# Chunks of x 64 bytes further apart, for gate and fill, in an attention and MoE kernel

## The chip, the cores and the metric

The kernel runs on one core of one Trainium2 chip. The metric is the device time of one execution in microseconds (us): 1310.79 us before the change, the median of three runs (1310.79 to 1315.36). An execution with the hardware profiler on gives the profile. Its engines are PE (matmul; PEld is its weight load), DVE, ACT, POOL and SP.

## The reference

```
phi(x)  = [exp(p), exp(-p)],  p = x @ w_phi - max|x @ w_phi|
kv      = phi(k)^T v,  z = sum phi(k)              # per batch and head
attn    = phi(q) kv / (phi(q) z + 1e-6)            # 8 x 8 heads, 576 x 64
x       = attn as 4608 tokens x 512                # then the MoE part
xn      = x / rms(x) * rms_g
out     = (silu(xn @ w_gate) * (xn @ w_val)) @ w_out   # 512 -> 1536 -> 512
```

All of it is float32. Every product of two matrices is split into a high and a low part of each factor and made of three products: high x high, high x low, low x high.

## The kernel before, in words

The work has three stages that overlap a little. In *attention* pairs of heads go through `front`, `mid`, `back` and `last`; `last` stores x, transposed, to the DRAM tensor `xs` (512 x 4608). x has 512 rows, so a contraction over them takes four chunks of 128 partitions: NC = 4.

*Fill* uses PE time between and after the attention work. `fill` takes a block of 256 tokens (TF; 18 blocks), splits it into high and low parts in the tile `xo`, and makes the first three of the twelve columns of 128 of gate and of val without the division by rms: six outputs a block, called units. Each is a sum of twelve products of 256 columns (L482): four chunks c, three products each. They go to DRAM by way of the tile `fo`.

*Gate* works on blocks of 512 tokens (T; NB = 9). `prep` makes x / rms * g, and `parts` splits it into the tile `xb`, high and low parts of four chunks. `gv` makes the other nine columns j of gate and of val: for each of two a sum of twelve products of 512 columns (L625). `hidden` applies silu on ACT and the product on DVE, and stores to `hs`.

*The output stage* loads `hs` as `ht` in groups of 256 tokens, forms seven sums and differences of quarter blocks (a11, a12, s1 to s4, a22), splits them, and makes seven products (L805), each a sum over kp = 0 to 5 of three products of 256 columns with the output weights `wh0` to `wh5` and `wl0` to `wl5`. These are split by `split_o` near the end of gate; `wh5` is the last.

In a matmul call the first operand is loaded as weights (stationary) and the second streams through (moving). In fill and gate the moving operand is a chunk of x; in the output stage it is a weight tile, and the stationary one a part of `ht`.

What is behind what: each engine runs its instructions in order. The order is set when the program is built, by the order of the code, by `late()`, which holds instructions back, and by a scheduler that simulates the program. Tiles lie in pools, one behind the other in a partition. When a pool is closed, the next ones take its place, and a new tile waits until the last reader of an old one beneath it is done. The two tiles `xb` lie in the pools `xo0` and `xo1`, and blocks take turns; blocks 0, 2, 4, 6 and 8 use `xo0`.

Addresses, by the built program, in bytes from the start of a partition: `xo` starts at 60192 and 68384, `xb` at 68384 and 101152, all 32 mod 256. A chunk of `xb` is 512 floats or 2048 bytes, one of `xo` 256 floats or 1024 bytes, so all chunks start at 32 mod 256. The weights of fill and gate start at 32 mod 256 too, and so do the stationary operands of the output stage. `wh0` to `wh3` and `wl0` to `wl3` start at 224 mod 256, `wh4`, `wl4`, `wh5` and `wl5` at 32. In attention the moving operands `wh` and `wl` of L319 to L321 start at 96 mod 256, and `qh` and `ql` of L423 at 32 for the first half of the columns and at 160 for the second, each against stationary operands at 32.

Of the kernel before, what the change touches and what calls it, by code (L numbers as in the profile page):

```python
# [9 lines left out]
F32R = mybir.dt.float32r  # L10
# [48 lines left out]
def _split(nc, hi, lo, x, hi_copy=None, lo_eng=None):  # L59
    (hi_copy or nc.scalar.copy)(hi, x)  # L60
    (lo_eng or nc.vector).tensor_tensor(lo, x, hi.bitcast(F32), ALU.subtract)  # L61
# [21 lines left out]
def kernel(ctx: ExitStack, tc: tile.TileContext, q, k, v, w_phi,  # L83
# [5 lines left out]
    NC, NJ = DM // 128, DF // 128  # L89
# [8 lines left out]
    T = 512  # L98
    NB = N // T
    TF = 256  # L100
# [65 lines left out]
        return ri  # L166

    def parts(bk, x, ri):
        xhl = xops[bk % len(xops)].tile([128, 2, NC, T], F32R, name="xb")
        for c in range(0, NC, 2):  # L170
            _split(nc, *(a[:, c:c + 2] for a in (xhl[:, 0], xhl[:, 1], x)), lo_eng=nc.gpsimd)
        return xhl[:, 0], xhl[:, 1], ri
# [7 lines left out]
    @contextmanager  # L180
    def late():

        ins = nc.cur_bb.bb.instructions
        n = len(ins)
        with ExitStack() as es:
            for eng in LATE:
                for i in reversed(ins[-300:]):
                    if i.engine == eng and i.name not in waiting:
                        es.enter_context(tc.issue_after(i))
                        break  # L190
            yield
        waiting.update(i.name for i in nc.cur_bb.bb.instructions[n:])
# [3 lines left out]
    xfp = a_ctx.enter_context(tc.tile_pool(name="a_xf", bufs=2))  # L196
# [269 lines left out]
    blocks = list(range(N // TF))  # L466

    def fill(bk, x):
        xhl = xfp.tile([128, 2, NC, TF], F32R, name="xo")
        xx = dict(h=xhl[:, 0], l=xhl[:, 1])  # L470
        with late():
            for c in range(0, NC, 2):
                _split(nc, *(a[:, c:c + 2] for a in (xx["h"], xx["l"], x)))

        def unit(j, wi):
            js = slice(j * 128, (j + 1) * 128)
            fp = ps_s.tile([128, 512], F32, name="sm") if ended else ps_f.tile([128, T], F32, name="fp")
            i = 0
            for c in range(NC):
                a, al = wf1[wi][0][:, c, js], wf1[wi][1][:, c, js]  # L480
                for w, x in ((a, "h"), (a, "l"), (al, "h")):
                    nc.tensor.matmul(fp[:, 0:TF], w, xx[x][:, c], start=(i == 0), stop=(i == 3 * NC - 1))  # L482
                    i += 1
            o = xfp.tile([128, TF], F32, name="fo", bufs=6)
            nc.scalar.copy(o, fp[:, 0:TF])
            (nc.scalar if tail else nc.sync).dma_start(out=gvv[j][:, wi, bk * TF:(bk + 1) * TF], in_=o)
        return [lambda j=j, wi=wi: unit(j, wi) for j in range(J1) for wi in range(2)]
# [13 lines left out]
    def landed():  # L501
        if here:
            units.extend(fill(*here.pop(0)))
# [63 lines left out]
    def own(name, bufs=1):  # L567
        return g_ctx.enter_context(tc.tile_pool(name=name, bufs=bufs, reuse_waits="tile"))
# [3 lines left out]
    xops = [own("xo0"), xo1]  # L572
# [106 lines left out]
    split_gv(1)  # L679
    raw = raw_load(0, 0)  # L680
    xb = {0: parts(0, x0, ri0)}

    LAST = [*range(JL, JN), 4, 5, *range(4)]
    for bk in range(NB):
        for n, j in enumerate(LAST if bk == NB - 1 else range(JN)):
            gv(bk, j)
            m, k = divmod(n, JN // J1)
            if k == 1:
                with late():
                    gv_raw(bk, m, raw)  # L690
            if k == 2 and (m + 1 < J1 or bk + 1 < NB):
                raw = raw_load(bk, m + 1) if m + 1 < J1 else raw_load(bk + 1, 0)
            if n == 0 and bk + 1 < NB:
                xn = fetch(bk + 1)
            if n == 2 and bk + 1 < NB:
                with late():
                    rin = prep(bk + 1, xn, *((ps_f, "fp") if bk else (ps_g, "gp")))
                xb[bk + 1] = parts(bk + 1, xn, rin)
            if bk and n % 2 == 0 and decs:
                decs.pop(0)()  # L700
            if wot and n % 4 == 0:
                with late():
                    wos_ops.append(split_o(len(wos_ops), rg, wot))
                wot = None
            if not decs and not wot and len(wos_ops) < PRE and n % 4 == 1:
                wot = fetch_o(len(wos_ops))
# [170 lines left out]
```

## Time and profile before

| | |
|---|---|
| median of three runs | 1310.79 us |
| the profiled execution | 1314.92 us, span 1313.0 us |
| mean granted TensorE clock | 0.996 of full speed |
| PE busy | 1277.2 us (97%) |
| DVE, ACT, POOL busy | 840.1 us (64%), 706.1 us (54%), 626.7 us (48%) |
| gate's first and last product (L625) | 499.7 and 1046.3 us |
| fill's first and last product (L482) with val weights | 196.3 and 623.5 us |

The busy time of an engine counts every moment in which at least one of its instructions runs. Products are pipelined: one is still draining while the next streams in, so that the mean duration of one (389 ns with 512 columns) is longer than the time from one start to the next. The chain of waits is followed back from the last instruction, and what it says of a line is time that passed on that line alone. A tile's name stands without its number in these rows: `wh<-wc` may be any of the six.

### The profile page before, as it was taken

Reading aid. Unit: us, or ns where it says so; the run is one execution under the profiler, and the core shown is the slowest. Engines: PE = TensorE matmul, PEld = TensorE weight load, DVE = VectorE, ACT = ScalarE, POOL = GpSimd, SP = SyncE. Lnnn points to the kernel's source line nnn. Section 1 sums busy time; section 2 is a strip of 40 time slices with the busy share of each in tenths; the row PEclk is TensorE's granted clock in tenths of the full one; section 3 lists DMA queues with packets and bytes.
Section 4 is the critical chain, followed back from the end, with each engine's and each line's share of the span. In section 5 each row is a group of like instructions: output and inputs, shape, how many; then the busy total and the mean of one; then the engine's idle time right before and its main releaser. Section 6 shows DMA issues by size and latency. Waiting matters only on the chain.

```text
span 1313.0 us, 24159 instructions
## 1 busy us (share of the span) xinstructions
PE 1277.2 (97%) x8886; PEld 1188.5 (91%) x8886; DVE 840.1 (64%) x1228; ACT 706.1 (54%) x1472; POOL 626.7 (48%) x580
## 2 busy tenths in 40 slices
PE   7989999999999998999999999999999999999998
PEld 7989999999999897999888888888888899999998
DVE  7989888787788962320245645644545786687773
ACT  6978887787778874543243443442332444444442
POOL 4666655565555854200414223223211277776774
PEclk9999999999999999999999999999999999999999
DMA  5545565566656436643446435434425544445541
GB/s 162 132 128 149 163 183 147 149 179 173 179 158 176 126 95 187 201 153 118 147 142 208 147 130 196 150 126 158 144 87 164 182 144 149 143 131 160 159 129 48
DMA packets 198228, 197.12 MB, mean 150 GB/s; under 512 B 69024, under 2 KB 154912, under 8 KB 198112
## 3 DMA queue, kind: packets, MB, share of 16 engines
q1 hardware_dynamic: 169024, 172.26, 43.5%
q10 hardware_dynamic: 29088, 23.34, 5.9%
q8 instruction: 70, 1.15, 0.4%
q14 instruction: 46, 0.38, 0.1%
HBM read 126.04 MB, written 69.50 MB: 149 GB/s over the span
## 4 chain that ended last, share of the span: by engine, by line
PE 80%; DVE 8%; DMA 5%; ACT 3%; issue 2%; SPq 1%; POOL 1%; ACTq 0%; DVEq 0%; POOLq 0%
PE gp L625 18%; PE gq L625 15%; PE gd L805 6%; PE gy L805 6%; PE gz L805 6%; PE sm L482 6%; PE acc L359 4%; PE fp L482 4%; PE sm L423 3%; PE fp L805 3%; PE fp L423 2%; PE pp L321 2%; PE pp L319 2%; DVE mx L323 2%; PE pp L320 1%
## 5 line engine op out<-in xcount | busy, mean ns | idle before, releaser
L388 POOL TENSOR_TENSOR ql<-eq,qh 128x256 fp32r<-128x256 f32 x256 | 218.2, 884 | 54.3 <-issue 31.1
L608 DVE TENSOR_TENSOR h<-sl,gp 128x512 f32<-128x512 f32 x81 | 55.4, 685 | 169.5 <-PE gp L625 159.2
L625 PE MATMUL gp<-xb,wv 128*128 128x512 f32 x648 | 157.8, 389 | 0.0
L625 PEld LDWEIGHTS gp<-xb,wv 128*128 128x128 f32 x648 | 121.1, 188 | 24.7
L625 PE MATMUL gq<-xb,wg 128*128 128x512 f32 x576 | 139.0, 389 | 0.0
L54 POOL TENSOR_TENSOR wa<-raw,wa 128x192 f32<-128x192 f32 (+1 forms) x112 | 67.1, 622 | 137.7 <-DVE wa L52 70.4
L61 POOL TENSOR_TENSOR xb<-x,xb 128x1024 fp32r<-128x1024 f32 x18 | 45.9, 2572 | 180.5 <-ACT xb L60 180.5
L359 PE MATMUL acc<-vm,ek 128*128 128x65 f32 x1024 | 130.3, 269 | 0.0
L625 PEld LDWEIGHTS gq<-xb,wg 128*128 128x128 f32 x576 | 108.1, 188 | 22.5
L359 PEld LDWEIGHTS acc<-vm,ek 128*128 128x128 f32 x1024 | 126.5, 192 | 0.5 <-ACT ek L346 0.4
L323 DVE TENSOR_REDUCE mx<-pp 128x4 f32<-128x512 f32 (+1 forms) x160 | 100.7, 630 | 30.3 <-PE pp L321 29.0
L384 ACT ACTIVATE qh<-sm 128x512 fp32r<-128x512 f32 (+1 forms) x192 | 97.0, 505 | 0.0
L319 PE MATMUL pp<-wh,th 128*128 128x256 f32 x288 | 88.9, 310 | 4.8 <-ACT th L60 1.5
L606 ACT ACTIVATE sl<-gq 128x512 f32<-128x512 f32 x72 | 42.7, 593 | 84.3 <-PE gq L625 80.3
L383 ACT ACTIVATE eq<-sm 128x512 f32<-128x512 f32 x128 | 78.3, 612 | 14.8 <-PE sm L372 11.6
L321 PE MATMUL pp<-wh,tl 128*128 128x256 f32 x288 | 84.5, 300 | 0.1
L320 PE MATMUL pp<-wl,th 128*128 128x256 f32 x288 | 81.5, 284 | 0.0
L625 PE MATMUL gp<-xb,fv 128*128 128x512 f32 x324 | 77.8, 389 | 0.0
L346 ACT ACTIVATE ek<-yk 128x512 f32<-128x512 f32 x128 | 75.1, 647 | 1.1 <-DVE yk L326 1.1
L154 POOL TENSOR_TENSOR ss<-ss,sq 128x512 f32<-128x512 f32 x27 | 34.8, 1289 | 79.7 <-ACT sq L153 79.7
L625 PEld LDWEIGHTS gp<-xb,fv 128*128 128x128 f32 x324 | 60.8, 188 | 12.6
L625 PE MATMUL gq<-xb,fg 128*128 128x512 f32 x288 | 69.2, 389 | 0.0
(210 smaller groups left out, 3802.9 us busy)
## 6 DMA issues: line engine op xcount, KB each, us to landing
hs<-h SPq DMA_DIRECT2D x108, 256.0 KB
ht<-hs SPq DMA_DIRECT2D x18, 1536.0 KB
gvr<-gvs SPq DMA_DIRECT2D x27, 512.0 KB
rc<-di SPq DMA_DIRECT2D x32, 288.0 KB
x<-xs ACTq DMA_DIRECT2D x18, 512.0 KB
x<-xs SPq DMA_DIRECT2D x9, 1024.0 KB
gvs<-fo ACTq DMA_DIRECT2D x70, 128.0 KB
kt<-in_k_dram SPq DMA_DIRECT2D x32, 256.0 KB
```

The costliest lines, as they stand in the source:

```text
L319: nc.tensor.matmul(o, th[:, cs], wh, start=True, stop=False)
L320: nc.tensor.matmul(o, th[:, cs], wl, start=False, stop=False)
L321: nc.tensor.matmul(o, tl[:, cs], wh, start=False, stop=True)
L323: nc.vector.tensor_reduce(mx[:, 0:2 * m], pp[:, 0:2 * m], axis=AX.X, op=ALU.max, apply_absolute_value=True)
L346: nc.scalar.activation(e[h][:, sg], y["k", h], AF.Exp, scale=1.0 - 2.0 * sg)
L359: nc.tensor.matmul(acc[:, sg, h], e[h][:, sg, j], vm[:, h, j], start=False, stop=(h == 1 and j == T0 - 1))
L383: nc.scalar.activation(ei[:, sg], yi, AF.Exp, scale=1.0 - 2.0 * sg)
L384: nc.scalar.activation(hi[:, sg], yi, AF.Exp, scale=1.0 - 2.0 * sg)
L388: nc.gpsimd.tensor_tensor(lo[:, sg, cs], ei[:, sg, cs], hi[:, sg, cs].bitcast(F32), ALU.subtract)
L482: nc.tensor.matmul(fp[:, 0:TF], w, xx[x][:, c], start=(i == 0), stop=(i == 3 * NC - 1))
L625: nc.tensor.matmul(gp[:, 0:T], w, e[:, c], start=(i == 0), stop=(i == 3 * NC - 1))
L805: nc.tensor.matmul(place[n], a[:, kp], w[:, o], start=(first and kp == 0 and i == 0), stop=(kp == KP - 1 and i == 2), skip_group_check=True)
```

## The change

Both tiles of x's parts get rows that are 16 floats longer, and only the first T or TF columns of a row are used.

```
     def parts(bk, x, ri):
-        xhl = xops[bk % len(xops)].tile([128, 2, NC, T], F32R, name="xb")
+        xhl = xops[bk % len(xops)].tile([128, 2, NC, T + 16], F32R, name="xb")[:, :, :, 0:T]
...
     def fill(bk, x):
-        xhl = xfp.tile([128, 2, NC, TF], F32R, name="xo")
+        xhl = xfp.tile([128, 2, NC, TF + 16], F32R, name="xo")[:, :, :, 0:TF]
```

The chunks are then 2112 and 1088 bytes apart and start at 32, 96, 160 and 224 mod 256. A high and a low chunk of the same c have the same residue. `xb` grows by 512 bytes and so does each of the two `xo`; what lies behind moves by 512 or 1024, and no other tile changes its address mod 256. No instruction is added or taken away; the splits write two stretches where they wrote one.

The tile `xb` of the last block lay at 101152 to 117536 and now lies at 101664 to 118560. `wh5` stays at 117536, so now it begins under the end of `xb`. This moves instructions at one place, the step from gate to the output stage. On ACT the rows there (`sl` is gate's silu, `s4h` and `a22h` are splits of the first output group):

```order
 L606 ACTIVATE sl_12364<-gq_12338 128x512
 L606 ACTIVATE sl_12397<-gq_12371 128x512
-L60 CAST wh5_12540<-wc_12530 128x768
-L60 CAST wh5_12540<-wc_12531 128x1024
 L606 ACTIVATE sl_12428<-gq_12402 128x512
 L606 ACTIVATE sl_12434<-gvr_12369 128x512
 L606 ACTIVATE sl_12465<-gq_12439 128x512
+L60 CAST wh5_12540<-wc_12530 128x768
+L60 CAST wh5_12540<-wc_12531 128x1024
 L60 CAST s4h_12574<-st_12559 128x768
 L60 CAST a22h_12578<-ht_12512 128x768
```

The two casts of `wh5` move behind the last three silu rows of gate, and the first of them waits for PE. On DVE the two subtractions for `wl5` move in the same way. On PE, in the second product of the first output group (`wh_12540` and `wl_12541` are `wh5` and `wl5`, `wh_12524` and `wl_12525` are `wh4` and `wl4`; `fp` is the first product, `gy` the second, `gz` the fourth):

```order
 L805 MATMUL gy<-wh_12163,a12l 128x256
 L805 MATMUL gy<-wh_12524,a12h 128x256
+L805 MATMUL fp<-wh_12540,a11h 128x256
 L805 MATMUL gy<-wl_12525,a12h 128x256
 L805 MATMUL gy<-wh_12524,a12l 128x256
 L805 MATMUL gy<-wh_12540,a12h 128x256
+L805 MATMUL gz<-wh_11646,s3h 128x256
+L805 MATMUL gz<-wl_11647,s3h 128x256
+L805 MATMUL gz<-wh_11646,s3l 128x256
```

The first product's part with `wh5`, which stood right behind its part with `wh4`, now comes 13 products later, and products of `gz` are drawn ahead of the part with `wl5`. Apart from these places the order on every engine is what it was.

## The prediction

> **What bounds the kernel now.** I read the page first, then the chain of waits in order of time, then the timeline of PE at a few places. Two lines of the page give the frame.
>
> ```profile
> span 1313.0 us, 24159 instructions
> PE 1277.2 (97%) x8886; PEld 1188.5 (91%) x8886; DVE 840.1 (64%) x1228; ACT 706.1 (54%) x1472; POOL 626.7 (48%) x580
> PE 80%; DVE 8%; DMA 5%; ACT 3%; issue 2%; SPq 1%; POOL 1%; ACTq 0%; DVEq 0%; POOLq 0%
> ```
>
> PE is busy for 97% of the span, and 80% of the chain that ended last is PE. So the question is what one product costs. The durations in the page overlap, since products are pipelined; the chain of waits counts each stretch of time once, and gives the pace from one start to the next. Its columns are start, length, what, and how many products.
>
> ```profile
> 508.58 7.30 DMA wc<-wvs
> 566.34 8.62 PE sm L482 x72
> 901.66 2.72 PE gp L625 x12
> 937.47 2.72 PE gq L625 x12
> 1150.78 4.16 PE gy L805 x36
> ```
>
> A gate product (L625, 512 columns) costs 2.72 / 12 = 226.7 ns, a fill product (L482, 256 columns) 8.62 / 72 = 119.7 ns, and an output product (L805, 256 columns too) only 4.16 / 36 = 115.6 ns. The last two have the same shape, 128x128 against 256 columns. What differs between them is where the operands lie. By the built program's allocation every stationary operand of these three lines starts at 32 mod 256 bytes, and so does every chunk of x in gate and fill. In the output stage the moving operand of kp 0 to 3 starts at 224 mod 256, that of kp 4 and 5 at 32. One output of six kp, three products each, on the timeline of PE (start, duration): the rows are the first products of kp 0, 2, 3 and 4, and of the next output.
>
> ```profile
> 1208.85 0.28 PE L805 MATMUL gy<-wh,a12h 128*128 128x256 f32 x1
> ...
> 1209.55 0.28 PE L805 MATMUL gy<-wh,a12h 128*128 128x256 f32 x1
> ...
> 1209.89 0.28 PE L805 MATMUL gy<-wh,a12h 128*128 128x256 f32 x1
> ...
> 1210.23 0.28 PE L805 MATMUL gy<-wh,a12h 128*128 128x256 f32 x1
> ...
> 1210.93 0.28 PE L805 MATMUL gy<-wh,s2h 128*128 128x256 f32 x1
> ```
>
> From 1209.55 to 1210.23 six products at 224 take 0.68 us: 113.3 ns each. If the twelve at 224 cost 113.3 and the six at 32 cost the 119.7 of fill, the eighteen cost 2.08 us, and 1208.85 to 1210.93 is 2.08. So I read two paces for 256 columns, 113.3 and 119.7 ns, 6.4 ns apart, and the start address of the moving operand tells them apart. Gate and fill run wholly at the slow one.
>
> Two more residues can be seen in the attention stage. L319 to L321 move wh and wl, which start at 96; L423 moves qh and ql, whose second half of columns (288) starts at 160. The stationary operands start at 32 here as well.
>
> ```profile
> 63.15 0.28 PE L320 MATMUL pp<-wl,th 128*128 128x256 f32 x1
> 63.62 0.28 PE L321 MATMUL pp<-wh,tl 128*128 128x256 f32 x1
> ...
> 64.40 0.28 PE L320 MATMUL pp<-wl,th 128*128 128x256 f32 x1
> 64.86 0.28 PE L321 MATMUL pp<-wh,tl 128*128 128x256 f32 x1
> ...
> 173.63 0.29 PE L423 MATMUL fp<-qh,kv0h 128*128 128x288 f32 x1
> 174.30 0.30 PE L423 MATMUL fp<-qh,kv0l 128*128 128x288 f32 x1
> ```
>
> The first two rows are four steps apart, 0.47 / 4 = 117.5 ns, and so are the next two, 0.46 / 4 = 115 ns. So 96 lies between the two paces. The last two rows are five steps apart: 134 ns for 288 columns. From 256 to 512 columns the slow pace rises by 107 ns, 0.418 ns a column; 32 columns more than 256 make 133.1 at the slow pace and 126.7 at the fast one. So 160 is slow. My reading: 32 and 160 are slow, 96 and 224 fast (96 perhaps in part).
>
> **The change, part by part.** The pads make a chunk 2112 bytes in gate (8 x 256 + 64) and 1088 in fill (4 x 256 + 64), so the four chunks start at 32, 96, 160 and 224 mod 256, in the high and in the low part alike. The weights stay at 32. Each chunk is the moving operand of three products.
>
> *Gate.* 9 blocks x 9 j x 2 x 12 = 1944 products, half of them on chunks 1 and 3. No row shows 512 columns at another residue. The nearest is the 6.4 ns between 119.7 and 113.3 of 256 columns; if the difference grew with the columns it would be 12.8, and if chunk 1 or 3 took the 117.5 of the rows at 63 us, 2.2. I take 6.4 (220.3 ns a product), since the fast and the slow pace of 256 and the slow ones of 288 and 512 columns differ by a fixed amount and the rate per column. 972 x 6.4 ns = 6.2 us; by 2.2 ns 2.1 us. From 560 us on PE is never idle until the output stage, so all but the few products ahead of that count. What could be late next is a block's parts: the waits of PE list one wait of gate, on weights, and none on xb.
>
> ```profile
> PE gp L625 <- POOL wg L61: 0.5, 1, 0.5
> PE fp L482 <- ACT fo L485: 5.6, 4, 2.1
> ```
>
> *Fill.* 18 blocks x 6 units x 12 = 1296 products, 648 on chunks 1 and 3. Where they lie is in the windows of L482 (window, its length, PE busy with them and count):
>
> ```profile
> 520.00:560.00 40.00, 27.08 (x217) 26.77 (x218) 1.00 0.63 201
> 560.00:600.00 40.00, 38.77 (x320) 38.68 (x320) 1.00 0.46 147
> 600.00:640.00 40.00, 22.66 (x187) 22.41 (x185) 1.00 0.46 153
> ```
>
> 724 come after 520 us, where PE ends the chain with little else: 362 x 6.4 ns = 2.3 us. The other 572 are spread through attention and its end, where the chain has DVE, ACT and the 7.30 us of a weight load that PE doesn't shorten: 286 x 6.4 = 1.8 us at most, nothing at least, and I take half, 0.9.
>
> *Parts.* ACT, POOL and DVE now write two stretches of 512 (or 256) columns where they wrote one of 1024 (or 512), in as many instructions. The nearest rows are a split that reads six stretches of 128 and the one that is changed:
>
> ```profile
> L60 ACT CAST a11h<-ht 128x768 fp32r<-128x768 f32 x18 | 15.1, 840 | 24.8 <-PE fp L805 20.5 <-DMA ht<-hs 4.3
> L60 ACT CAST xb<-x 128x1024 fp32r<-128x1024 f32 x18 | 18.7, 1050 | 16.0 <-DVE x L165 14.2 <-DMA gvs<-fo 1.8
> L61 POOL TENSOR_TENSOR s2l<-st,s2h 128x768 fp32r<-128x768 f32 x18 | 33.5, 1859 | 56.1 <-ACT s2h L60 56.1
> L61 POOL TENSOR_TENSOR xb<-x,xb 128x1024 fp32r<-128x1024 f32 x18 | 45.9, 2572 | 180.5 <-ACT xb L60 180.5
> ```
>
> 1.09 against 1.03 ns a column on ACT, 2.42 against 2.51 on POOL: between nothing and 6%, at most 0.06 us a cast, made a block ahead. I cost it at nothing; a wait of L625 on xb would show that the cover is gone.
>
> *The switch to the output stage.* xb of the last block is now 512 bytes longer and starts 512 later, so that its end lies under wh5, the last output weights. Their two casts on ACT now wait for the last gate product, and their two subtractions on DVE follow; PE's order was changed for it: 28 output products stand ahead of the first that reads wh5.
>
> ```profile
> 1043.84 2.88 PE L625 MATMUL gp<-xb,wv 128*128 128x512 f32 x12
> 1046.56 0.28 PE L805 MATMUL fp<-wh,a11h 128*128 128x256 f32 x1
> ...
> 1040.17 1.05 ACT L60 CAST wh<-wc 128x1024 fp32r<-128x1024 f32 x1 [0.34 <-DVE wc L661]
> 1046.45 0.83 ACT L60 CAST s4h<-st 128x768 fp32r<-128x768 f32 x1
> 1040.74 2.09 DVE L61 TENSOR_TENSOR wl<-wc,wh 128x768 fp32r<-128x768 f32 x2
> ```
>
> 28 x 115.6 ns = 3.2 us of cover; the first cast (768 columns, by the s4h row 0.83) is through about 0.85 us after the last gate product ends at 1046.72, and wl5's first half about 1 us later, while PE wants it 37 products on, 4.3 us. Queued behind on ACT are s4h and a22h, 1.9 us later than before, which PE reads some 10 us later. Cost nothing; were the 28 products not to cover it, 0.8 to 4 us.
>
> A rule of the Trainium skill speaks against all of the gain. The page "SBUF — State Buffer", section "Who interferes with whom", says that PE and ACT never wait for anyone at the memory's ports, and "TensorE: Matmul & The Clock Gate", Part 2, that the moving operand and the weight load have read ports of their own. By these no start address would matter, and the sum would be 0 instead of 9.4 us; the 113.3 against 119.7 above speaks against it, as far as one shape in two stages can.
>
> The sum: 6.2 + 2.3 + 0.9 = 9.4 us. The profiled execution took 1314.92 us for its span of 1313.0, the median of the runs is 1310.79, 4.1 less; the gain is in products that all runs have, so I take it from the median: 1301.4 us. With 2.2 ns a product and nothing from attention: 2.1 + 0.8 = 2.9 us, 1307.9.
>
> **The rivals.** *One chunk alone.* If 96 is as slow as 32 here (the run at 63 us went at 117.5) and only 224 is fast, half is left: 486 x 6.4 + 181 x 6.4 + 143 x 6.4 / 2 = 4.7 us, 1306.1. Against it: the run at 64 us went at 115.
>
> *Three chunks.* If what counts is that the moving chunk and the weights have the same residue, or that products in a row take turns, 160 gains too: 1458 x 6.4 = 9.3, fill 543 x 6.4 = 3.5 and 429 x 6.4 / 2 = 1.4, together 14.2 us, 1296.6. The 134 ns at 160 speaks against it.
>
> *No effect.* The 6.4 ns may belong to something else in which the stages differ (fill moves one tile of x, the output stage twelve tiles of weights, and by then ACT and DVE do less) and not to addresses: 1310.8. The Trainium skill's rule on ports, above, gives the same.
>
> *Slower.* A change of residue between products may cost. In the output rows kp 0 and 1, after the step from 32 to 224, take 1209.55 - 1208.85 = 0.70 us against 0.68 of kp 2 and 3. At up to 0.01 us a change and four changes in each of 162 gate and 108 fill outputs, 1080 changes cost 10.8 us; if none of the residues gained, 1321.6. It decides from 0.009 us a change on, where it eats up the 9.4. Against it: the 2.08 us of eighteen products is accounted for without it.
>
> **How the numbers follow.** Two chunks 0.47 (1299 to 1308, three quarters of it near 1301.4), one chunk 0.15, three 0.13, none 0.16, slower 0.09. The runs of before lie between 1310.79 and 1315.36; I take 0.5%, 6.6 us, as what a measurement can tell. Faster by more than that is below 1304.2: 0.36 of two chunks, 0.13, and 0.06 of the others' scatter, 0.55. Slower than 1317.3: 0.09. The rest, 0.36, is the same. The range runs from a little below three chunks to a little above none, 1294 to 1312: it leaves out the slower case and the edges, 0.15 to 0.2.
>
> **What would show it.** In the chain, twelve gate products take 2.68 us instead of 2.72 (6 x 226.7 + 6 x 220.3); 2.70 with one chunk, 2.64 with three, 2.72 with none, more with the slower case. 72 fill products take 8.39 instead of 8.62. The output products stay at 4.16 for 36. The prediction is wrong if 512 columns don't have the fast pace that 256 have, if the last gate product is followed by a wait of L805 on ACT wh, or if fill's gain comes back as a longer wait at the 7.30 us load.

## The result, and the profile after

The changed kernel takes 1318.92 us (median of 6 runs, 1317.41 to 1321.13), the kernel before, in runs beside it, 1310.87 (6 runs, 1310.78 to 1315.36). The ratio is 1.0051, interval 1.0037 to 1.0066: slower by half a per cent, where 1301.4 us were predicted and 1294 to 1312 was the range.

Three lines of the page after: the span, the busy time of the engines, and the shares of the chain that ended last.

```profile
span 1315.5 us, 24160 instructions
PE 1282.6 (98%) x8886; PEld 1184.9 (90%) x8886; DVE 841.2 (64%) x1228; ACT 705.6 (54%) x1472; POOL 628.1 (48%) x580
PE 82%; DVE 7%; DMA 5%; ACT 3%; issue 2%; SPq 1%; POOL 0%; ACTq 0%; DVEq 0%; POOLq 0%
```

PE issues the same 8886 products and is busy 5.4 us longer. Its share of the chain grew from 80 to 82%. The span grew by only 2.5 us, less than the medians did by 8.1. The two profiled executions lie differently to their medians: that of before, 1314.92 us, is 4.1 above, that of after, 1317.55, is 1.4 below. So the comparison goes by stage. The chain of waits after, with the columns start, length, what, and how many products:

```profile
502.22 7.35 DMA wc<-wvs
...
560.08 8.51 PE sm L482 x72
...
664.99 2.78 PE gp L625 x12
...
1065.86 4.16 PE gy L805 x36
```

The 72 fill products went from 8.62 to 8.51 us: faster, by half of what was predicted (8.39). The twelve gate products went from 2.72 to 2.78 us, where 2.68 was predicted. A product of 512 columns now takes 231.7 ns instead of 226.7. The output stage stayed at 4.16.

The products of L625 grouped by form show the length of gate as a whole (least, median and greatest duration in ns, then first and last start). Before:

```profile
L625 PE MATMUL gp<-xb,wg x72: 388/389/501, 499.7 to 642.2; 128*128 128x512 f32 x72
L625 PE MATMUL gp<-xb,wv x648: 388/389/398, 500.2 to 1046.3; 128*128 128x512 f32 x162
```

And after:

```profile
L625 PE MATMUL gp<-xb,wg x72: 388/395/628, 493.2 to 635.6; 128*128 128x512 f32 x72
L625 PE MATMUL gp<-xb,wv x648: 387/394/404, 493.6 to 1048.8; 128*128 128x512 f32 x162
```

Before, gate runs from 499.7 to 1046.3, 546.6 us; after from 493.2 to 1048.8, 555.6. That is 9.0 us more, and 1944 products at 5.0 ns more are 9.7. Where gate starts scatters from 492.8 to 509.9 us over the runs told of below, with an attention stage of the same instructions; so one execution can hide the loss in its start, as this one does.

A later stretch scatters much less. It goes from the first of fill's last 660 products to the first product of the output stage, holds 1876 products of gate, and has one order in both kernels. It starts, in the timeline of PE (start, duration), before:

```profile
538.47 0.28 PE L482 MATMUL sm<-xo,fg 128*128 128x256 f32 x1
```

And after:

```profile
532.59 0.28 PE L482 MATMUL sm<-xo,fg 128*128 128x256 f32 x1
```

The output stage begins at 1046.56 before and at 1049.00 after (rows in the prediction and below). So the stretch takes 508.09 us before and 516.41 after, 8.3 more, close to the 8.1 of the medians. Three kernels told of below in which x and its weights keep the same residue (all chunks at 32; x and weights both at 96; the output weights moved) take 508.08 to 508.09 as well.

The waits of PE after (engine and line that waited, what for, us in total, times, longest) show that nothing new keeps PE from its work:

```profile
PE fp L482 <- ACT fo L485: 3.2, 3, 1.8
...
PE gp L625 <- POOL wg L61: 0.6, 1, 0.6
...
PE gp L625 <- ACT wg L60: 0.2, 1, 0.2
```

L625 doesn't wait for `xb`. The parts cost what they did (busy time of the group, mean ns of one, idle time before them):

```profile
L60 ACT CAST xb<-x 128x1024 fp32r<-128x1024 f32 x18 | 18.7, 1049 | 15.5 <-DVE x L165 13.7 <-DMA gvs<-fo 1.8
L61 POOL TENSOR_TENSOR xb<-x,xb 128x1024 fp32r<-128x1024 f32 x18 | 46.4, 2600 | 181.6 <-ACT xb L60 181.6
```

And at the switch to the output stage the timeline after (start, duration) has the cast of `wh5` right behind the last gate products, done 1.2 us before PE reads it:

```profile
1046.22 2.94 PE L625 MATMUL gp<-xb,wv 128*128 128x512 f32 x12
1049.00 0.28 PE L805 MATMUL fp<-wh,a11h 128*128 128x256 f32 x1
...
1052.21 0.27 PE L805 MATMUL fp<-wh,a11h 128*128 128x256 f32 x1
...
1049.20 1.78 ACT L60 CAST wh<-wc 128x768 fp32r<-128x768 f32 x2 [0.67 <-PE gp L625]
```

So the loss that the trace shows is the pace of the gate products. In one gate output the steps from a start to the next start are, over the four chunks at 32, 96, 160 and 224 mod 256: 226 236 228, 232 233 234, 232 233 231, 229 233 233 ns, 2780 in all, and they repeat from output to output.

### The profile page after: what moved, and what is told of

The parts are those of the page before. It is cut to its first block, busy times and chain, and to the rows that moved or that the text cites. A ratio compares the mean times of both kernels' runs of the same rounds, so it can differ in the third digit from the quotient of the medians.

```text
span 1315.5 us, 24160 instructions
## 1 busy us (share of the span) xinstructions
PE 1282.6 (98%) x8886; PEld 1184.9 (90%) x8886; DVE 841.2 (64%) x1228; ACT 705.6 (54%) x1472; POOL 628.1 (48%) x580
## 4 chain that ended last, share of the span: by engine, by line
PE 82%; DVE 7%; DMA 5%; ACT 3%; issue 2%; SPq 1%; POOL 0%; ACTq 0%; DVEq 0%; POOLq 0%
PE gp L625 18%; PE gq L625 15%; PE gd L805 6%; PE gy L805 6%; PE gz L805 6%; PE sm L482 6%; PE acc L359 5%; PE fp L482 4%; PE sm L423 3%; PE fp L805 3%; PE fp L423 2%; PE pp L321 2%; PE pp L319 2%; PE pp L320 2%; PE sm L372 2%
## 5 line engine op out<-in xcount | busy, mean ns | idle before, releaser
L625 PE MATMUL gp<-xb,wv 128*128 128x512 f32 x648 | 160.8, 394 | 0.0
L625 PEld LDWEIGHTS gp<-xb,wv 128*128 128x128 f32 x648 | 121.2, 188 | 27.8
L625 PE MATMUL gq<-xb,wg 128*128 128x512 f32 x576 | 141.9, 394 | 0.0
L625 PEld LDWEIGHTS gq<-xb,wg 128*128 128x128 f32 x576 | 108.2, 188 | 25.3
L625 PE MATMUL gp<-xb,fv 128*128 128x512 f32 x324 | 79.4, 394 | 0.0
L625 PEld LDWEIGHTS gp<-xb,fv 128*128 128x128 f32 x324 | 60.9, 188 | 14.2
L625 PE MATMUL gq<-xb,fg 128*128 128x512 f32 x288 | 70.6, 394 | 0.0
```

What stands on the lines that cost most here:

```text
L625: nc.tensor.matmul(gp[:, 0:T], w, e[:, c], start=(i == 0), stop=(i == 3 * NC - 1))
```

## The experiments

Two theories stood at first. *Own price*: each start address has a price for 512 columns, which needn't be that of 256, and the three new residues are dearer. *Turns*: any residue alone is no worse than before, and what costs is that the residue changes between products. Later ones are told where they came up. All ratios are to the kernel before in runs on the same chip.

**Every residue by itself.** Eight kernels keep the chunks together, as before, and move the whole tile: all of x's chunks in gate and fill have one residue. K is 0, 16, 32 and 48 floats in the first four.

```diff
-        xhl = xops[bk % len(xops)].tile([128, 2, NC, T], F32R, name="xb")
+        xhl = xops[bk % len(xops)].tile([128, 2 * NC * T + 64], F32R, name="xb")[:, K:K + 2 * NC * T].rearrange("p (a c t) -> p a c t", a=2, c=NC)
...
-        xhl = xfp.tile([128, 2, NC, TF], F32R, name="xo")
+        xhl = xfp.tile([128, 2 * NC * TF + 64], F32R, name="xo")[:, K:K + 2 * NC * TF].rearrange("p (a c t) -> p a c t", a=2, c=NC)
```

At 32, which also moves the end of `xb` under `wh5` as the change does:

> The tiles xb and xo are 256 bytes longer, and their chunks lie as in the kernel before: back to back, all at 32 mod 256. What stays of the change is only that the tiles behind move, so that wh5 begins under the end of xb again. Theory 'turns cost' (a product is slower when the residue of the moving operand changes around it): pace as before, 2.72 us for twelve gate products and 8.62 for 72 of fill. Theory 'residue' (each residue has its own pace against weights at 32): the same. Theory 'placement or switch' (the loss comes from moved tiles or from wh5 waiting for the last gate product): the time is up by about 8 us as in the changed kernel, with the pace as before.

At 96:

> Chunks back to back, all moved by 64 bytes: every chunk of gate and fill at 96 mod 256, weights at 32. Theory 'turns cost': the residue never changes between products of a stage, so 2.72 us for twelve gate products as before, and the time as before. Theory 'residue': the changed kernel's products on chunk 1 went at 232 to 234 ns, so about 2.79 us for twelve gate products, some 11 us more than before in gate. The prediction's own reading (96 is a fast residue): 2.64 us.

At 160:

> Every chunk of gate and fill at 160 mod 256, weights at 32. Theory 'turns cost': 2.72 us for twelve gate products. Theory 'residue': 2.79 (the changed kernel's chunk 2 went at 232 to 233 ns). The prediction's reading (160 is a slow residue like 32): 2.72, which does not tell it from 'turns cost'.

At 224:

> Every chunk of gate and fill at 224 mod 256, weights at 32, as the moving operand of kp 0 to 3 in the output stage. Theory 'turns cost': 2.72 us for twelve gate products. Theory 'residue' by the changed kernel's chunk 3 (229 to 233 ns): 2.78. The prediction's reading (224 is fast): 2.64 for gate, and 8.16 for 72 fill products (113.3 ns each, as in the output stage).

The chain of waits at 32:

```profile
567.44 8.62 PE sm L482 x72
...
672.01 2.72 PE gp L625 x12
```

The chain of waits at 96:

```profile
564.06 8.48 PE sm L482 x72
...
581.95 8.16 PE sm L482 x72
...
667.84 2.75 PE gp L625 x12
```

The chain of waits at 160:

```profile
581.93 8.54 PE sm L482 x72
...
669.14 2.79 PE gp L625 x12
```

The chain of waits at 224:

```profile
550.67 4.24 PE sm L482 x36
...
583.32 8.16 PE sm L482 x72
...
669.08 2.80 PE gp L625 x12
```

For 256 columns 224 is fast in most places, 113.3 ns a product, as was read in the output stage; the 36 products from 550.67 on go at 117.8. For 512 columns the same residue is slow, 233.3 ns. Each of the three new residues is dearer in gate than 32. The ratios: 1.0007 (0.9995 to 1.0019), 1.0022 (1.0003 to 1.0041), 1.0085 (1.0053 to 1.0117) and 1.0052 (1.0025 to 1.0078). *Own price* is shown as far as these go. It doesn't account for all: the mean of the four residues' own paces is 230.4 ns, and the changed kernel has 231.7. The first run also settles that moving `xb`'s end under `wh5` costs nothing.

Then the four residues between, K = 8, 24, 40 and 56 (64, 128, 192 and 0 mod 256); 128 and 192 in a single execution.

> All chunks at 64 mod 256, weights at 32: a difference of 32, half a step of the change. Theory 'difference' says only that the paces of gate and fill are again a fixed pair. If the pace goes smoothly with the difference, gate lies between 226.7 ns (difference 0) and 229 (64): 2.73 us for twelve. If the half step brings the operand to the start of a line of 64 bytes that it otherwise straddles, gate drops by a line, some 6.4 ns: 2.64 us.

> All chunks at 128 mod 256: a difference of 96 from the weights. Smooth: between 229 (64) and 232.5 ns (128), 2.77 us for twelve gate products. Straddled lines: 2.64 us as with the difference 32.

> All chunks at 192 mod 256: a difference of 160 from the weights. Smooth: between 232.5 (128) and 233.2 ns (192), 2.79 us for twelve gate products. Straddled lines: 2.64 us.

> All chunks at 0 mod 256: a difference of 224 from the weights. Smooth: between 233.2 (192) and 226.7 ns (0), 2.76 us for twelve gate products. Straddled lines: 2.64 us.

The chain of waits at 64:

```profile
563.55 8.48 PE sm L482 x72
...
627.71 2.80 PE gq L625 x12
```

All eight together, with d the residue of x less that of the weights (32), mod 256, and paces from the chain:

| x at | d | gate, 512 columns, ns | fill, 256 columns, ns | ratio (interval) |
|---|---|---|---|---|
| 32 | 0 | 226.7 | 119.7 | 1.0007 (0.9995 to 1.0019) |
| 64 | 32 | 233.3 | 116.7 to 117.8 | 1.0103 (1.0063 to 1.0142) |
| 96 | 64 | 229.2 | 117.8 or 113.3 | 1.0022 (1.0003 to 1.0041) |
| 128 | 96 | 233.3 | 120.0 | one execution, 1334.88 us |
| 160 | 128 | 232.5 | 118.6 | 1.0085 (1.0053 to 1.0117) |
| 192 | 160 | 234.2 | 117.4 to 118.6 | one execution, 1328.05 us |
| 224 | 192 | 233.3 | 113.3, once 117.8 | 1.0052 (1.0025 to 1.0078) |
| 0 | 224 | 233.3 | 118.3 | 1.0080 (1.0051 to 1.0110) |

The two single executions stand beside a median of 1315.14 us before. At d = 32 twelve gate products take 2.80 us; a smooth course gave 2.73 there and straddled lines 2.64, so neither of these two theories holds. For 512 columns the kernel before has the one fast place of eight. For 256 columns the same place is next to the slowest.

**The change in halves.** Its first hunk alone (gate) and its second alone (fill):

> The change in gate alone: chunks of xb at 32, 96, 160, 224, fill as before. 'Residue': the loss of the changed kernel is gate's, 1944 products x 5.0 ns (2.78 against 2.72 us for twelve) = 9.7 us, so ratio 1.0074 and 2.78 us in the chain. 'Placement': the loss stays below that and fill_only shows a loss too.

> The change in fill alone: chunks of xo at the four residues, xb as before. 'Residue': 8.51 instead of 8.62 us for 72 products, 1.5 ns each; 724 products after 520 us make 1.1 us and the 572 before up to 0.9: ratio 0.9985 to 0.9992. With gate_only the two add up to the changed kernel's 1.0051. 'Turns cost': fill is slower than before, ratio above 1.000.

The chain of waits of gate alone:

```profile
576.04 8.62 PE sm L482 x72
...
632.04 2.78 PE gq L625 x12
```

And of fill alone:

```profile
562.40 8.52 PE sm L482 x72
...
662.40 2.72 PE gq L625 x12
```

Gate alone is slower, 1.0083 (1.0054 to 1.0111), fill alone faster, 0.9966 (0.9946 to 0.9986). Their product, 1.0049, agrees with the 1.0051 of the whole change: the two halves add up. So they do in the stretch from fill's last 660 products to the output stage, 508.09 us before: gate alone takes 517.55, 9.5 more, and fill alone 1.1 less, if four gate products that run ahead of the stretch there are counted in. The whole change made it 8.3 more.

**Fill at 224, gate as before.** Only the second of the two edits above, with K = 48:

> Each stage at the residue that was its fastest in the four runs with one residue: fill's xo at 224, gate's xb at 32 as before. 'Residue': 8.16 us for 72 fill products and 2.72 for twelve of gate; 724 products after 520 us x 6.4 ns = 4.6 us, and of the 572 before (3.7 us) nothing to all: ratio 0.9937 to 0.9965. If fill's pace is hidden by something else the ratio stays at 1.000.

Its chain of waits:

```profile
575.16 8.48 PE sm L482 x72
...
639.07 2.72 PE gq L625 x12
```

Fill takes 8.48, not the 8.16 that the same fill had with gate at 224 too. The ratio is 0.9977 (0.9955 to 0.9999). So 256 columns at d = 192 have two paces, 117.8 and 113.3 ns, and the kernel with all chunks at 224 has both. The residue alone doesn't say which. The two kernels differ in gate's residue, and fill runs between gate products.

**The difference or the address.** An unused tile of 64 bytes ahead of the others moves x and the weights of gate and fill to 96 alike, so that d stays 0. In the output stage it moves the stationary operands to 96, and the weights of kp 4 and 5 with them, so that their d stays 0. The weights of kp 0 to 3 stay at 224, so that their d goes from 192 to 128. (What was expected took all of them to stay.)

```diff
-    eps = gl.tile([128, 1], F32, name="eps")
+    eps = gl.tile([128, 1], F32, name="eps"); gl.tile([128, 16], F32, name="gap")
```

> An unused tile of 64 bytes at the start of the partition moves every tile of the first pools by 64: x's chunks AND the weights of gate and fill at 96, the difference 0 as before. Theory 'difference' (what counts is the moving operand's residue less the weights'): 2.72 us for twelve gate products, 8.62 for 72 of fill, and output products change, since their weights stay at 224 while the stationary operands go to 96 (difference 128). Theory 'absolute' (only the moving operand's own residue counts): 2.75 for gate and 8.48 for fill as with all chunks at 96, and the output stage as before.

Its chain of waits:

```profile
564.03 8.62 PE sm L482 x72
...
668.61 2.72 PE gp L625 x12
...
1046.57 4.27 PE gy L805 x36
```

Gate and fill keep 2.72 and 8.62 to the digit, although every address in them is another; the output stage, where twelve products of eighteen have another difference now, goes from 4.16 to 4.27, although none of these twelve moving operands was moved. What counts is the difference between the moving and the stationary operand's start, as far as one shift of 64 bytes can show it. The ratio, 1.0060 (1.0036 to 1.0084), is the output stage's: 2268 products at 3.06 ns more are 6.9 us, 0.53%.

**Turns without a difference.** In this kernel x takes turns as in the change, but the weights `fg` take the same turns, so that their own products all have d = 0. `fv`, `wg` and `wv` stay at 32.

```diff
-    wf1 = [[wfp.tile([128, NC, J1 * 128], F32R, name=f"f{n}{i}") for i in range(2)] for n in "gv"]
+    wf1 = [[wfp.tile([128, NC, J1 * 128 + 16 * (n == "g")], F32R, name=f"f{n}{i}")[:, :, 0:J1 * 128] for i in range(2)] for n in "gv"]
...
-        xhl = xops[bk % len(xops)].tile([128, 2, NC, T], F32R, name="xb")
+        xhl = xops[bk % len(xops)].tile([128, NC, 2 * T + 16], F32R, name="xb")[:, :, 0:2 * T].rearrange("p c (a t) -> p a c t", a=2)
```

(and `xo` alike.)

> x's chunks take turns as in the changed kernel (in gate and fill), and the chunks of the weights fg of the first three gate columns take the same turns; the weights fv, wg and wv stay at 32. So products with fg have the difference 0 to their own weights, though residues change every three products; the others have 0, 64, 128, 192 in turn. 'Difference alone': fg as before the change, 2.72 us for twelve in gate; the others 2.78 as in the changed kernel. 'Turns cost by themselves': fg well above 2.72 too. 'What counts is the weights loaded while a product streams, which are the next product's': one product of three has 192 at the border of chunks, (9 x 226.7 + 3 x 233.2) / 12 = 228.3 ns, 2.74 us.

The timeline of PE, one output of `fv` and the one of `fg` behind it (start, duration):

```profile
838.62 2.94 PE L625 MATMUL gp<-xb,fv 128*128 128x512 f32 x12
841.39 2.94 PE L625 MATMUL gq<-xb,fg 128*128 128x512 f32 x12
844.17 2.94 PE L625 MATMUL gp<-xb,fv 128*128 128x512 f32 x12
```

From 841.39 to 844.17 the twelve products of `fg` take 2.78 us, as long as those with differences, and the mean of 27 such outputs is 231.5 ns a product. So d = 0 is not enough for the fast pace: here it costs 4.8 ns a product more. Turns aren't shown to be the reason, since each output of `fg` also stands between outputs whose differences aren't all 0, and gate takes time to settle. In the kernel with fill alone moved, where all of gate is at d = 0, these rows follow fill's last products:

```profile
618.90 2.70 PE L625 MATMUL gp<-xb,wg 128*128 128x512 f32 x11
621.44 2.88 PE L625 MATMUL gp<-xb,wv 128*128 128x512 f32 x12
624.16 0.62 PE L625 MATMUL gq<-xb,wg 128*128 128x512 f32 x2
```

The first eleven products take 2.54 us, 230.9 ns each, the next twelve 2.72, 226.7 each. An output of `fg` has only twelve. So turns aren't told apart from a pace that is carried over from the products before. The ratio is 1.0062 (1.0041 to 1.0083). That the next product's weights, which are loaded during a product, are what the difference is taken to falls short as well: it gave 2.74.

**The output stage's two residues.** The prediction split 4.16 us into twelve fast products at 224 and six slow ones at 32. If that is right, `wh4`, `wl4`, `wh5` and `wl5` moved to 224 make all eighteen fast.

```diff
-        wh = pool.tile([128, 7, DH], F32R, name=f"wh{kp}")
-        wl = pool.tile([128, 7, DH], F32R, name=f"wl{kp}")
+        wh = (kp >= PRE and pool.tile([128, 48], F32, name="gap"), pool.tile([128, 7, DH], F32R, name=f"wh{kp}"))[1]
+        wl = (pool.tile([128, 7, DH], F32R, name=f"wl{kp}"), kp >= PRE and pool.tile([128, 16], F32, name="end"))[0]
```

> Only the last output weights (kp 4 and 5) are moved, from 32 to 224 mod 256, so that all output products have the difference 192; gate and fill as before. 'Difference': 113.3 ns for all of them, 4.08 instead of 4.16 us for 36, 756 products x 6.4 ns = 4.8 us, ratio 0.9963. If the pace of the output stage is set by something else: 4.16 and 1.000.

With fill at 224 besides:

> As the last one, and fill's xo at 224 too; gate as before. Output 4.8 us; fill at 113.3 ns (8.16 us for 72) 4.6 us after 520 us and up to 3.7 before, at the 117.8 seen with xo alone moved (8.48) 1.4 and up to 1.1. Ratio 0.990 to 0.995. It also shows once more which of its two paces fill takes at the difference 192.

The chain of waits of the first:

```profile
562.74 8.62 PE sm L482 x72
...
1045.25 4.24 PE gy L805 x36
```

And of the second:

```profile
563.20 8.48 PE sm L482 x72
...
1044.70 4.24 PE gy L805 x36
```

All products at 224 make the stage slower, 117.8 ns instead of 115.6, and the run 1.0040 (1.0024 to 1.0055); 2268 at 2.2 ns are 5.0 us, 0.38%. With fill at 224 it is 1.0020 (1.0006 to 1.0035). 117.8 is the slower of the two paces that fill showed at the same d. The kernel before shows both in its output stage. Its timeline of PE at the start of the output stage: the first rows of kp 4 of the first output, of kp 0 and kp 1 of the second, and of its kp 4.

```profile
1047.97 0.28 PE L805 MATMUL fp<-wh,a11h 128*128 128x256 f32 x1
...
1048.69 0.29 PE L805 MATMUL gy<-wh,a12h 128*128 128x256 f32 x1
...
1049.05 0.28 PE L805 MATMUL gy<-wh,a12h 128*128 128x256 f32 x1
...
1050.07 0.28 PE L805 MATMUL gy<-wh,a12h 128*128 128x256 f32 x1
```

The first output starts at 1046.56, a row that the prediction shows. Its twelve products at 224 take 1.41 us up to 1047.97: 117.5 ns. The six at 32 follow, at 120.0. After them the same kind of product at 224 needs 1.02 us for nine from 1049.05: 113.3. So the stream at d = 192 comes out of this gate stage, with d = 0, in its slow pace, and it is fast behind six products of another residue; in the two kernels without these six it stays slow to the end. What gate leaves behind matters too. In the changed kernel the first output starts at 1049.00, with the same operands, and the first row of its kp 4 is

```profile
1050.37 0.28 PE L805 MATMUL fp<-wh,a11h 128*128 128x256 f32 x1
```

Its twelve products at 224 take 1.37 us, 114.2 ns each, with no product at 32 ahead of them in the stage. They are fast in gate alone moved as well, where gate is the same, and slow in every kernel here with gate at d = 0 and these products at d = 192. So the pace hangs on what ran before; which property of it counts isn't shown.

**Can fill be brought into the fast pace?** Fill's high parts at 224 and its low parts at 32, so that two of three products have d = 192 and one has 0. The tile is `[128, 2 * (NC * TF + 16) + 96]`, begun at float 48, with 16 unused floats between high and low parts.

> In fill alone, x's high parts lie at 224 mod 256 and its low parts at 32, weights at 32: products go 224, 32, 224, two thirds at the difference 192 and one third at 0, as in the output stage but in turns of one. Gate and output as before. 'A product at 32 kicks the stream into the fast pace' (as the output stage, where six of eighteen at 32 stand before twelve at 113.3): (2 x 113.3 + 119.7) / 3 = 115.4 ns, 8.31 us for 72, ratio about 0.996. 'Turns cost by themselves': at or above the 117.8 of all at 224, 8.48 us or more, ratio 0.998 or above. If the paces of the two residues simply mixed with the slow one of 224: 118.4 ns, 8.53.

Its chain of waits:

```profile
561.63 8.48 PE sm L482 x72
...
661.35 2.72 PE gq L625 x12
```

8.48 again, 117.8 ns, so turns of single products don't bring it about. The ratio is 0.9960 (0.9939 to 0.9981), 1309.83 us beside 1315.65: the ratio of the first theory, but without its pace. This kernel, fill alone (0.9966) and fill at 224 (0.9977) beat the kernel before by 0.2 to 0.4%; their intervals overlap, so they aren't told apart.

## Why the prediction was wrong

*The gate term failed.* It took 6.4 ns off 972 products, a difference between rows of 256 columns, for 512 columns of which no row showed a second residue. Its ends, 2.2 and 12.8 ns, were both gains. Measured: the residues 96, 160 and 224 cost 2.5, 5.8 and 6.6 ns more than 32, and the mixture 5.0 more on all 1944: +9.7 us in place of -6.2. Gate alone moved lost 9.5 us in the stretch that scatters little. Of these four residues the best for 512 columns is the worst for 256, and the other way round. A loss of the same 6.4 ns belonged at the other end: nothing in the trace excluded it. The prediction did name the point on which it hung, "if 512 columns don't have the fast pace that 256 have".

*The split of 4.16 us failed, although its arithmetic closed.* 12 x 113.3 + 6 x 119.7 is 2.08 us, but the pace belongs to the stream and its past and not to each product's residue: with all eighteen at 224 the stage took 117.8 ns a product. A sum that closes with two paces fitted to it is weak evidence. Rows that speak against the split were in the trace of before, and the first of them was quoted: from 1046.56 us on, twelve products at 224 at 117.5 ns.

*Fill* went the predicted way, and its pace by less: 118.2 ns in place of 116.5. Fill alone is 4.5 us faster (1.8 to 7.1), where 3.2 were predicted; 724 to 1296 products at 1.4 ns explain 1.0 to 1.8. All three kernels with fill alone moved gained more (3.0 to 5.3 us) than their pace gives (1.0 to 2.5); this lies inside the interval of fill at 224 and at the edge of the other two. In the stretch of fill's last 660 products the trace shows about what the pace gives: 1.1 us for fill alone, 1.5 for fill at 224 (506.58 against 508.09). Whether the rest comes from ahead of it, where executions scatter, or is noise is open.

*The parts, and the switch,* cost nothing, as costed: casts of 1049 and 2600 ns against 1050 and 2572, no wait on `xb`, and 1.0007 for the kernel that moves `xb`'s end alone.

*The rivals.* No rival was right whole. The slower one gave 1321.6 and the time came within 2.7 us of it, partly by luck. It charged 40 ns to each output of gate and fill alike; an output of gate became 60 ns longer and one of fill 18 ns shorter. That changes of residue cost of themselves, as it held, isn't shown. The rival of three chunks named the relation that counts, moving chunk against weights, with the wrong sign for gate. The rival without effect had beside it the Trainium skill's page "SBUF — State Buffer", section "Who interferes with whom". What the prediction drew from its sentence that PE never waits on anyone, that no start address would matter, doesn't hold against these runs: the distance between PE's own two operands alone moves a product from 226.7 to as much as 234.2 ns. PE may wait on nobody else and still be held up by itself.

*The sum after the fact:* gate +9.7, fill -1.1 to -1.9, the rest nothing: +7.8 to +8.6 us. The medians say +8.1, the ratio 6.7 (4.9 to 8.7).

## What to carry to other kernels

Where PE is the bound, the distance mod 256 between the starts of moving and stationary operand is worth up to 3.3% of a 512-column fp32r product here. It has to be tried by the stage and by the width: what is best for one width was among the worst for the other. A mixture isn't the mean of its residues (231.7 against 230.4 ns here), and a stream's pace hangs on what ran before it too, so a constant difference is the simpler thing to try. Read the pace from starts in the chain, output by output, before and after; a pace read in one stage is no price for another shape. Where a change touches two stages, run each half alone: here one half was a gain that the other hid.

## What was not expected of the hardware

- A stream of equal products can have two stable paces. 256 columns at d = 192 ran at 113.3 or 117.8 ns, one kernel's whole output stage at 117.8. What ran before plays a part: behind gate the output stage began at 117.5 ns a product in the kernel before and at 114.2 in the changed one. At d = 64 both were seen in one run (8.48 and 8.16 us for 72).
- Steps repeat in short cycles: at 96, 512 columns go 226, 229, 232 ns over and over; at 224, 231 and 236. With the four residues in turn the cycle is one output long.
- The number of columns doesn't fix the time: 512 columns took, at a granted clock of 0.99 to 1.00, 226.7 to 234.2 ns, 256 columns 113.3 to 120.0, each by the distance of its operands.
- Still open: why the order of the residues differs with the width, what sets which of the two paces a stream falls into, why a mixture costs more than the mean of its residues, and whether turns cost of themselves.
